# Low parts of four weight blocks: from TensorE products to a GpSimd subtraction and a VectorE addition

## The chip, the cores and the metric

One core of a Trainium2 chip. The metric is the device time of one execution in microseconds (us), the median of several runs. The engines are TensorE (PE in the profile, its weight loads PEld), VectorE (DVE), ScalarE (ACT), GpSimd (POOL) and SyncE (SP), which issues all loads and stores.

## What is computed

Masked attention for 8 batches, 8 heads, 576 tokens, head size 64 (heads 0 to 3 see the last 32 positions, heads 4 to 7 the earlier positions with the same remainder by 32), and then a gated layer on the 512 joined features:

```python
attn = softmax(where(mask, q @ k.T / sqrt(D), -1e9)) @ v
x = attn.transpose(0, 2, 1, 3).reshape(B, S, H * D)
h = np.maximum(x @ w_in, 0.0)                   # 512 -> 1024
conv_out = sum(conv_w[k] * hp[:, k:k + S] for k in range(3))   # along the tokens
gate = 1.0 / (1.0 + np.exp(-conv_out))
return h * gate @ w_out                          # 1024 -> 512
```

The weights `w_in`, `conv_w` and `w_out` come as 64-bit floats.

## The kernel before, in words

**Two-part numbers.** Each operand of the large products is kept as a high part in a short form of fp32 (fp32r) and a low part, the rest. A product is then three TensorE instructions, high times high, low weight times high, high weight times low: `wih`, `wil` (from `w_in`) against `xh`, `xl` (lines 568), and `woh`, `wol` (from `w_out`) against `gh`, `gl` (line 634). Three such instructions of 512 columns are called a triple here.

**Weight blocks.** `convert` (from line 235) brings in the weights in eight blocks, c = 0 to 7: four of `w_in` (c 0 to 3), four of `w_out` (c 4 to 7), each of 1024 words in two halves b = 0, 1. SyncE loads the 64-bit words into a buffer `ws` (two of them, taken in turn). A clamp (line 282, on GpSimd or VectorE), ScalarE's `abs` (283), VectorE's `ts` and `stt` (284, 285) make a fp32 `t` out of the upper words, in place; ScalarE rounds it to the high part `wh` (287); VectorE's `ts` and `stt` (294, 296) make the `tail` out of the lower words in a buffer `wl`. The low part is t - wh + tail, and `SPLIT_W` says for each block how it is formed:

- "a" (lines 307 to 313): op `whole` on TensorE, three products into a PSUM bank (`eye` by t, `negr`, the negative unit matrix, by wh, and `eyer` by the tail), and ScalarE's `evict` to SBUF.
- "q" (lines 315 to 320): op `less` on TensorE, two products (`negr` by wh, `eyer` by the tail), and VectorE's `vadd` (line 319) adds t out of SBUF to the bank and writes the low part.

`SPLIT_W` is "aaqqqaqq": of the last four blocks, 4, 6 and 7 are "q" and 5 is "a".

**Attention.** A unit is one batch and one pair of heads, 32 in all. VectorE and ScalarE do the softmax; VectorE turns its result (line 448, `STREAM_TRANSPOSE`) for the product with v. From unit 4 on, TensorE's scores of unit n (line 370) and values of unit n-1 (line 471) are one op, a `visit`, written here as visit n. ScalarE and VectorE then take `xh` (504) and `xl` (529) out of PSUM.

**The layer.** For each of nine groups g of 512 tokens and each of eight column blocks f, `mm1` makes four triples into a bank, and `conv_gate` follows: ScalarE's `relu` (581), VectorE's scaling or ScalarE's (596, 593), two `conv` (602), ScalarE's `tanh` (605), VectorE's `gate` (606), ScalarE's `gh` (609), and `gl` (611) mostly on GpSimd. Three pairs of buffers, `hs` and `cs`, are taken in turn. `mm2` (634) makes eight triples for each of four output blocks m; output block m needs the low parts of weight block c = 4 + m.

**What sets the order.** All operations are first collected in a list, and `Plan.emit` (line 137) issues them in the order of a list of 2149 numbers written out by hand, `ORDER`. Each engine works in that order. `BANKS` gives the PSUM bank of each use; `FILLS` puts products of zeros ahead of a TensorE operation (line 654, each wide one 512 columns of bf16, each narrow one 256), which have no result. Before, there are 54 wide and 4 narrow ones, of which the last two stand ahead of visit 6.

Of the kernel before, what the change touches and what calls it, by code (L numbers as in the profile page):

```python
# [22 lines left out]
W = 32  # L23
# [4 lines left out]
SPLIT_W = "aaqqqaqq"  # L28
# [11 lines left out]
    "10322312121131300313023013133002101213101003123022131132231032011032302113023132013202133102103230210313023203022230113021332010"  # L40
)
ORDER = [
# [82 lines left out]
]  # L125
FILLS = {
    22: (0, 6, 1), 30: (0, 13, 1), 10: (0, 11, 0), 56: (5, 2, 0), 92: (0, 6, 0), 128: (3, 2, 0), 69: (4, 2, 1), 115: (2, 4, 1), 61: (0, 6, 0),
    317: (5, 2, 0),
}

class Plan:
# [3 lines left out]
    def op(self, engine, kind, fn, reads=(), writes=(), **more):  # L135
        self.ops.append((engine, kind, fn, tuple(reads), tuple(writes), more))
# [10 lines left out]
def tile_banded_attention_gated_mlp(ctx, tc, qkT, vw, w_in, conv, w_out, consts_in, more_in, out):  # L147
# [87 lines left out]
    def convert(src, kind, j):  # L235
# [28 lines left out]
        def block(x, b):  # L264
            return place(x, slice(b, b + 1))

        def four(x):
            return x.rearrange("p (c n) -> p c n", n=C)
# [499 lines left out]
```

## Time and profile before

| | |
|---|---|
| median of 3 runs | 502.88 us (502.09 to 503.33) |
| the profiled execution | 503.48 us |
| its span, first to last instruction | 501.6 us |
| TensorE, VectorE, ScalarE, GpSimd busy | 98%, 73%, 57%, 26% of the span |
| mean granted TensorE clock | 0.996 of full |

A row of a timeline gives the start, the duration, the engine, the line, the operation, the output and inputs by the program's names, the shape, how many instructions are merged in the row, and in brackets how long the engine had been idle and who ended it. TensorE products overlap: a product of 512 columns shows 0.39 us, and the next one starts about 0.23 after it.

### The profile page before, as it was taken

Reading aid. Unit: us, or ns where it says so; the run is one execution under the profiler, and the core shown is the slowest. Engines: PE = TensorE matmul, PEld = TensorE weight load, DVE = VectorE, ACT = ScalarE, POOL = GpSimd, SP = SyncE. Lnnn points to the kernel's source line nnn. Section 1 sums busy time; section 2 is a strip of 40 time slices with the busy share of each in tenths; the row PEclk is TensorE's granted clock in tenths of the full one; section 3 lists DMA queues with packets and bytes.
Section 4 is the critical chain, followed back from the end, with each engine's and each line's share of the span. In section 5 each row is a group of like instructions: output and inputs, shape, how many; then the busy total and the mean of one; then the engine's idle time right before and its main releaser. Section 6 shows DMA issues by size and latency. Waiting matters only on the chain.

```text
span 501.6 us, 15936 instructions
## 1 busy us (share of the span) xinstructions
PE 491.8 (98%) x6935; PEld 396.9 (79%) x6935; DVE 368.5 (73%) x655; ACT 283.4 (57%) x611; POOL 132.8 (26%) x216
## 2 busy tenths in 40 slices
PE   8799999999999999999999999999999999999996
PEld 4467767788888888888888888888888888888896
DVE  2999999877957687599768994888578755743730
ACT  4887687367535753367246653654376527745641
POOL 0200534031311340034303340323114303532430
PEclk9899999999999999999999999999999999999999
DMA  8766435420351314403045125004531120001001
GB/s 315 275 218 195 133 106 208 141 90 37 112 141 54 103 48 169 145 34 116 15 123 182 58 98 172 26 3 162 158 121 50 33 86 1 1 8 70 8 12 74
DMA packets 17350, 51.43 MB, mean 103 GB/s; under 512 B 2048, under 2 KB 2944, under 8 KB 17280
## 3 DMA queue, kind: packets, MB, share of 16 engines
q1 hardware_dynamic: 17280, 50.41, 29.5%
q8 instruction: 54, 0.88, 0.7%
q14 instruction: 16, 0.13, 0.1%
HBM read 40.97 MB, written 9.44 MB: 100 GB/s over the span
## 4 chain that ended last, share of the span: by engine, by line
PE 86%; DVE 7%; ACT 4%; issue 1%; POOL 1%; DVEq 0%; ACTq 0%
PE m L634 38%; PE m L568 36%; PE r L471 5%; PE r L370 4%; DVE misc L602 2%; PE m L654 2%; ACT t L405 1%; ACT t L446 1%; DVE ws L285 1%; ACT wa L283 1%; DVE misc L606 1%; DVE mx L392 1%; DVE wl L296 0%; DVE misc L596 0%; DVE sm L421 0%
## 5 line engine op out<-in xcount | busy, mean ns | idle before, releaser
L602 DVE SCALAR_TENSOR_TENSOR misc<-misc,cw 128x512 f32<-128x512 f32 (+26 forms) x256 | 131.2, 545 | 35.4 <-ACT misc L593 32.5
L634 PE MATMUL m<-gh,woh 128*128 128x512 f32 (+2 forms) x320 | 119.4, 373 | 0.0
L634 PE MATMUL m<-gl,woh 128*128 128x512 f32 (+2 forms) x320 | 117.8, 368 | 0.1
L634 PE MATMUL m<-gh,wol 128*128 128x512 f32 (+2 forms) x320 | 117.8, 368 | 0.0
L611 POOL TENSOR_TENSOR gl<-misc,gh 128x512 fp32r<-128x512 f32 (+1 forms) x70 | 86.1, 1234 | 107.9 <-ACT gh L609 104.1
L568 PE MATMUL m<-xh,wih 128*128 128x512 f32 x288 | 113.9, 395 | 0.0
L568 PE MATMUL m<-xh,wil 128*128 128x512 f32 x288 | 112.3, 390 | 0.0
L568 PE MATMUL m<-xl,wih 128*128 128x512 f32 x288 | 112.3, 390 | 0.0
L634 PEld LDWEIGHTS m<-gl,woh 128*128 128x128 f32 x320 | 60.2, 188 | 11.0 <-POOL gl L611 0.5
L634 PEld LDWEIGHTS m<-gh,woh 128*128 128x128 f32 x320 | 60.1, 188 | 10.3
L634 PEld LDWEIGHTS m<-gh,wol 128*128 128x128 f32 x320 | 60.1, 188 | 9.6
L581 ACT ACTIVATE misc<-m 128x512 f32<-128x512 f32 x72 | 42.5, 596 | 39.2 <-PE m L568 34.5
L593 ACT ACTIVATE misc<-misc,cw 128x383 f32<-128x383 f32 (+15 forms) x122 | 59.7, 523 | 8.2 <-POOL gl L611 4.2
L609 ACT CAST gh<-misc 128x512 fp32r<-128x512 f32 (+1 forms) x72 | 44.2, 618 | 35.1 <-DVE misc L606 34.8
L605 ACT ACTIVATE misc<-misc 128x512 f32<-128x512 f32 (+1 forms) x72 | 44.6, 628 | 33.5 <-DVE misc L602 33.4
L568 PEld LDWEIGHTS m<-xl,wih 128*128 128x128 f32 x288 | 54.1, 188 | 11.9 <-DVE xl L529 0.4
L568 PEld LDWEIGHTS m<-xh,wih 128*128 128x128 f32 x288 | 54.0, 188 | 11.8 <-ACT xh L504 0.2
L568 PEld LDWEIGHTS m<-xh,wil 128*128 128x128 f32 x288 | 54.1, 188 | 10.5
L583 POOL COPY misc<-carry 128x2 f32<-128x2 f32 x64 | 21.7, 347 | 152.2 <-DVE misc L606 91.7
L606 DVE SCALAR_TENSOR_TENSOR misc<-misc 128x512 f32<-128x512 f32 (+1 forms) x72 | 51.9, 725 | 11.7 <-ACT misc L605 11.1
L504 ACT CAST xh<-r 128x576 fp32r<-128x576 f32 (+13 forms) x56 | 23.5, 429 | 37.0 <-PE r L471 31.8
L641 ACT ACTIVATE misc<-m 128x512 f32<-128x512 f32 (+2 forms) x40 | 21.7, 556 | 39.6 <-PE m L634 39.1
(76 smaller groups left out, 494.3 us busy)
## 6 DMA issues: line engine op xcount, KB each, us to landing
qk<-in_dram SPq DMA_DIRECT2D x32, 592.0 KB, 5.0
v<-in_dram SPq DMA_DIRECT2D x32, 384.0 KB, 4.5
ws<-in_dram SPq DMA_DIRECT2D x14, 512.0 KB, 4.8
out_dram<-misc SPq DMA_DIRECT2D x28, 256.0 KB, 2.7
misc<-in_dram SPq DMA_DIRECT2D x2, 512.0 KB, 7.9
out_dram<-misc SPq DMA_DIRECT2D x4, 255.5 KB, 2.1
out_dram<-misc SPq DMA_DIRECT2D x3, 256.5 KB, 2.1
more<-in_dram SPq DMA_DIRECT2D x1, 320.0 KB, 5.2
```

Source lines behind the costliest of these rows:

```text
L471: nc.tensor.matmul(psV[64 * h:64 * h + 64, o:o + n_], v[W * c:W * c + W, h, j], tt[W * c:W * c + W, 64 * NBLK * h + a:64 * NBLK * h + z], ...
L504: op(A, "xh", lambda hi=hi, src=src: nc.scalar.copy(hi, src), ko, [("xh", hp, x) for x in halves], n=z - a)
L568: nc.tensor.matmul(ps, a[:, n, fs], x[:, c, N * x0:N * x0 + N], start=(n == 0 and m == 0), stop=(n == NC - 1 and m == 2))
L581: op(A, "relu", lambda: nc.scalar.activation(out=h[:, 2:N + 2], in_=ps, func=AF.Relu), [kp], [("h", hi)], n=N)
L583: op(G, "gcopy", lambda: nc.gpsimd.tensor_copy(out=h[:, 0:2], in_=carry[:, f, :]), [("carry", f)], [("h0", hi)], lock=True)
L593: op(A, "scale", lambda a=a, z=z: nc.scalar.activation(out=c_[:, a:z], in_=h[:, a + 1:z + 1], func=AF.Copy, scale=w1), kh + ["cw"], (kc if ...
L602: op(V, "conv", lambda k=k, wk=wk, a=a, z=z: nc.vector.scalar_tensor_tensor(out=c_[:, a:z], in0=h[:, a + k:z + k], scalar=wk, in1=c_[:, a: ...
L605: op(A, "tanh", lambda: nc.scalar.activation(out=c_[:, :n], in_=c_[:, :n], func=AF.Tanh, scale=0.5), kc, kc, n=n)
L606: op(V, "gate", lambda: nc.vector.scalar_tensor_tensor(out=c_[:, :n], in0=c_[:, :n], scalar=1.0, in1=h[:, 1:n + 1], op0=ALU.add, op1=ALU.m ...
L609: op(A, "gh", lambda: nc.scalar.copy(row(gh, g, f)[:, :n], c_[:, :n]), kc, [(k, "h") for k in keys], n=n)
L611: op(es, "gl", lambda: se.tensor_tensor(out=row(gl, g, f)[:, :n], in0=c_[:, :n], in1=row(gh, g, f)[:, :n].bitcast(F32), op=ALU.subtract), ...
L634: nc.tensor.matmul(ps, a[:, f, ms], row(y, g, f)[:, tok], start=(f == 0 and n == 0), stop=(f == NF - 1 and n == 2))
```

## The change

`SPLIT_W` becomes "aaqqpppp". For a block with "p", for each half, GpSimd subtracts wh from t into the buffer `wa` (op `wsub`, 512 columns, SBUF to SBUF), and VectorE adds the tail and writes the low part (op `tt`, 512 columns, SBUF to SBUF). No TensorE product, no PSUM bank and no ScalarE eviction is used. Op numbers stay the same, as each half had two operations before and has two now. `ORDER` is another order of the same 2149 numbers, on every engine and for the loads. `BANKS` has 120 entries in place of 128. `FILLS` now gives 91 wide and 5 narrow products of zeros.

```diff
-SPLIT_W = "aaqqqaqq"
+SPLIT_W = "aaqqpppp"
...
-            for b in bs:
+            if SPLIT_W[c] in "pd":
+                for b in bs:
+                    key = (kind, 2 * j + b)
+                    zb, eb = slice(512 * b, 512 * b + 512), [("WA", ia, b)]
+                    de, dn = (nc.gpsimd, G) if SPLIT_W[c] == "p" else (nc.vector, V)
+                    op(dn, "wsub", lambda zb=zb, b=b, de=de: de.tensor_tensor(out=four(af[:, zb]), in0=four(t[:, zb]), in1=block(wh, b).bitcast(F32), op=ALU.subtract),
+                       [("W", i, b), (key, "h")], eb, n=512, lock=True)
+                    op(V, "tt", lambda zb=zb, b=b: nc.vector.tensor_tensor(out=block(wlo, b), in0=four(af[:, zb]), in1=four(tail[:, zb].bitcast(F32)), op=ALU.add),
+                       eb + [("WL", il, b)], [(key, "l")], n=512, lock=True)
+                continue_ = True
+            else:
+                continue_ = False
+            for b in [] if continue_ else bs:
                 key = (kind, 2 * j + b)
                 mi = bank()
                 ps = psM[place_of(mi)]
...
 FILLS = {
-    22: (0, 6, 1), 30: (0, 13, 1), 10: (0, 11, 0), 56: (5, 2, 0), 92: (0, 6, 0), 128: (3, 2, 0), 69: (4, 2, 1), 115: (2, 4, 1), 61: (0, 6, 0),
-    317: (5, 2, 0),
+    22: (0, 12, 1), 30: (0, 17, 1), 10: (0, 11, 0), 56: (0, 10, 0), 69: (2, 1, 0), 82: (0, 15, 0), 370: (1, 1, 0), 331: (4, 4, 0), 195: (1, 1, 0),
+    301: (6, 2, 1), 451: (2, 1, 0), 417: (3, 13, 1), 376: (4, 3, 1),
 }
```

The first number of a `FILLS` entry is the TensorE operation that the zero-products precede: 331 is visit 7, 348 visit 8, 417 and 451 are triples of group 1, 370 and 376 triples of output block 1 of group 0. The parts of the orders that the prediction speaks of, counted from the two lists:

- VectorE, up to the transpose of unit 6 (op 324): the same operations as before and both additions of block 5 (218, 220).
- VectorE, up to the transpose of unit 7 (op 339): these two more; both additions of block 6 (257, 259) and three operations on block 7 (290, 291, 293: `ts`, `stt`, `ts`) now come after it.
- VectorE, from the last addition of block 5 (218) to the transpose of unit 6 (324): a sum, a reciprocal, two scalings, a `ts` of block 6, four `conv`, one `gate`.
- TensorE, up to visit 7: the same operations as before without the splits of blocks 4 and 5. Up to visit 8: also without those of block 6, and six triples of output block 2 (380 to 385) come after it.
- GpSimd: the second `wsub` of block 4 stands behind the clamp of block 5 and a `gl`; both `wsub` of block 5 behind the clamp of block 6, ahead of the `gl` of column block 3; those of blocks 6 and 7 behind all `gl` of group 0.
- SyncE: the loads of units 4 to 13 and of blocks 3, 5 and 7 change places among each other.

## Rows read from the trace of the kernel before

**Rows 1.** The page, busy time, share of the span and instructions of each engine.

```profile
PE 491.8 (98%) x6935; PEld 396.9 (79%) x6935; DVE 368.5 (73%) x655; ACT 283.4 (57%) x611; POOL 132.8 (26%) x216
```

**Rows 2.** By stretch: length, busy us (instructions) of PE, PEld, DVE, ACT, POOL, clock, DMA.

```profile
40.00:65.06 25.06, 24.93 (x370) 19.17 (x357) 24.83 (x42) 17.95 (x43) 7.65 (x9) 1.00 0.51 172
65.06:80.53 15.47, 14.88 (x211) 11.04 (x211) 15.47 (x24) 12.10 (x27) 4.18 (x4) 1.00 0.53 195
80.53:95.51 14.98, 14.87 (x213) 11.83 (x212) 14.88 (x24) 6.77 (x12) 5.19 (x5) 1.00 0.37 109
95.51:497.60 402.09, 402.09 (x5440) 335.19 (x5439) 283.37 (x517) 217.56 (x437) 110.20 (x183) 1.00 0.24 79
```

**Rows 3.** Timeline of TensorE, splits of blocks 4 and 5.

```profile
57.73 0.40 PE L316 MATMUL m<-woh,negr 128*128 128x512 f32 x1
...
58.20 0.40 PE L568 MATMUL m<-xh,wih 128*128 128x512 f32 x1
...
69.34 1.06 PE L309 MATMUL m<-ws,consts 128*128 128x512 f32 x2
...
71.23 0.50 PE L311 MATMUL m<-wl,eyer 128*128 128x512 f32 x1 [0.59 <-DVE wl L296]
...
72.93 0.39 PE L568 MATMUL m<-xh,wih 128*128 128x512 f32 x1
```

**Rows 4.** Timeline of TensorE, zero-products, visits 7 and 8, the last product.

```profile
42.76 0.71 PE L654 MATMUL m<-warm 128*128 128x512 bf16 x3
...
80.53 0.83 PE L370 MATMUL r<-qk 64*32 64x32 f32 x72
81.29 1.12 PE L471 MATMUL r<-tt,v 32*64 32x32 f32 x84
...
95.51 0.34 PE L370 MATMUL r<-qk 64*32 64x64 f32 x16
...
96.49 1.03 PE L471 MATMUL r<-tt,v 32*64 32x2 f32 x80
...
497.54 0.28 PE L634 MATMUL m<-gl,woh 128*128 128x258 f32 x1
```

**Rows 5.** Timeline of VectorE.

```profile
32.64 1.00 DVE L399 TENSOR_SCALAR mx<-mx 128x10 f32<-128x10 f32 x1
...
65.77 2.07 DVE L285 SCALAR_TENSOR_TENSOR ws<-ws,wa 128x1024 int32<-128x1024 int32 x1
...
69.96 1.21 DVE L296 SCALAR_TENSOR_TENSOR wl<-ws,wa 128x1024 fp32r<-128x1024 uint32 x1
...
75.22 0.82 DVE L421 TENSOR_REDUCE sm<-t 128x10 f32<-128x650 f32 x1
...
80.07 0.83 DVE L448 STREAM_TRANSPOSE tt<-t 128x640 f32<-128x640 f32 x1
...
83.44 0.68 DVE L611 TENSOR_TENSOR gl<-misc,gh 128x512 fp32r<-128x512 f32 x1
...
88.37 0.68 DVE L319 TENSOR_TENSOR wol<-ws,m 128x512 fp32r<-128x512 f32 x1
...
92.28 1.22 DVE L285 SCALAR_TENSOR_TENSOR ws<-ws,wa 128x1024 int32<-128x1024 int32 x1
...
93.62 0.68 DVE L294 TENSOR_SCALAR wa<-ws 128x1024 int32<-128x1024 int32 x1
94.22 0.84 DVE L448 STREAM_TRANSPOSE tt<-t 128x640 f32<-128x640 f32 x1
```

**Rows 6.** Groups of instructions of GpSimd, 54 to 86 us (busy, mean ns).

```profile
L611 POOL TENSOR_TENSOR gl<-misc,gh 128x512 fp32r<-128x512 f32 x7 | 9.5, 1365 | 19.7 <-ACT gh L609 19.7
...
L282 POOL TENSOR_SCALAR ws<-ws 128x1024 f32<-128x1024 f32 x2 | 2.8, 1408 | 2.9 <-DMA ws<-in_dram 2.9
```

**Rows 7.** Timeline of GpSimd, the clamp of block 6.

```profile
65.57 1.18 POOL L282 TENSOR_SCALAR ws<-ws 128x1024 f32<-128x1024 f32 x1 [2.94 <-DMA ws<-in_dram]
```

**Rows 8.** The chain that ended last: start, us, what; ten triples.

```profile
116.01 6.80 PE m L568 x30
```

More of the change, by code (lines that the diff above doesn't have):

```diff
@@ L39 @@
 BANKS = (
-    "10322312121131300313023013133002101213101003123022131132231032011032302113023132013202133102103230210313023203022230113021332010"
+    "013200200131032101031322131023112332103211300331300213201023012021300013102331021022310130122132301201121202331232231010"
 )
 ORDER = [
[82 rows of a table removed]
[82 rows of a table added]
 ]
 FILLS = {
-    22: (0, 6, 1), 30: (0, 13, 1), 10: (0, 11, 0), 56: (5, 2, 0), 92: (0, 6, 0), 128: (3, 2, 0), 69: (4, 2, 1), 115: (2, 4, 1), 61: (0, 6, 0),
-    317: (5, 2, 0),
+    22: (0, 12, 1), 30: (0, 17, 1), 10: (0, 11, 0), 56: (0, 10, 0), 69: (2, 1, 0), 82: (0, 15, 0), 370: (1, 1, 0), 331: (4, 4, 0), 195: (1, 1, 0),
+    301: (6, 2, 1), 451: (2, 1, 0), 417: (3, 13, 1), 376: (4, 3, 1),
 }
```

164 rows, old and new, of the table ORDER are left out of this document.

## The prediction

> **What bounds the kernel now.** The page first: TensorE is busy for 98% of the span [rows 1]. That says little about a single stage, so next the busy time by stretch [rows 2]. From 95.51 us on TensorE is never idle (402.09 of 402.09) while VectorE works 283.37 of the same 402.09, some 70%: TensorE alone sets the pace there. From 40 to 95.51 us both are nearly full (24.93 and 24.83 of 25.06; 14.88 and 15.47 of 15.47; 14.87 and 14.88 of 14.98). In that stretch two engines share the bound, and work taken from one of them is a gain only if the other lets it be. All the work that the change touches lies there, apart from its last block.
>
> The TensorE timeline shows what the old way costs: one `less` (two products) starts at 57.73 and the next product at 58.20, 0.47 us; the two `whole` of block 5 last from 69.34 to 72.93, 3.59 us, of which 0.59 is a wait for VectorE's tail [rows 3]. The fences of the argument are the visits: TensorE's visit n does the scores of unit n and the values of unit n-1, and its second half needs the transpose of unit n-1 from VectorE. Visit 7 starts at 80.53 and its values at 81.29, visit 8 at 95.51 and 96.49 [rows 4]; the transposes they need end at 80.07 + 0.83 = 80.90 and 94.22 + 0.84 = 95.06 [rows 5]. So at visit 7 TensorE has 0.39 us in hand, at visit 8 1.43 us.
>
> **The change, part by part.**
>
> *Taken from TensorE.* Six `less` and two `whole`: 6 x 0.47 + 3.59 = 6.4 us. Ahead of visit 7 stand two `less` and both `whole` (4.5 us), between visits 7 and 8 two `less` (0.94), after visit 8 two (0.94).
>
> *Taken from ScalarE.* Two evictions out of PSUM. ScalarE is not full in any stretch [rows 2], so nothing is counted; the cover is VectorE, which is full.
>
> *Given to VectorE.* Eight SBUF additions in place of six additions that read PSUM. The nearest row for the new form, the one subtraction of 512 columns that VectorE does between SBUF tiles, lasts 0.68 us, and the old PSUM addition 0.68 too [rows 5]. Instructions there follow each other 0.08 before the end of the last one (93.62 + 0.68 against 94.22), so an addition occupies 0.60, a `ts` of 1024 words 0.60, an `stt` 1.22 - 0.08 = 1.14. Six swaps cost nothing; the two additions of block 5, which replace ScalarE's evictions, cost 1.20 us of a full engine.
>
> *Given to GpSimd.* Eight subtractions. Seven of the same shape between 54 and 86 us took 1.37 us on average [rows 6], so 11 us in all; GpSimd works 7.65, 4.18 and 5.19 us in the three stretches [rows 2] and has room. In its queue the second subtraction of block 4 stands behind a clamp, and it now frees the buffer into which SyncE loads block 6, where the addition did before; I take that load 1 us later. The two of block 5 stand ahead of the `gl` of column block 3. Both delays end in slack: the clamp that took the load came at 65.57 [rows 7], and VectorE's first instruction on that block stands next to the reduction that starts at 75.22 [rows 5].
>
> *The shared access of VectorE and GpSimd.* At 65.57 GpSimd starts a clamp that lasts 1.18 [rows 7]; VectorE's `stt` that starts at 65.77 lasts 2.07 against 1.22 at 92.28 [rows 5], 0.85 more, so it stood until GpSimd was done. Of the nine long GpSimd instructions in that stretch [rows 6] this is the one large loss. The price of a new subtraction for VectorE lies between 0 (it falls beside VectorE work that reads PSUM) and its whole 1.37; I take 0.85 / 9 = 0.1, the mean over the nine, as they are the nearest rows: the same engine pair in the same stretch. Four subtractions lie ahead of visit 7: 0.4 us.
>
> The Trainium skill (SBUF - State Buffer, "Who interferes with whom") calls the pair of ports that these two engines share an exclusive lock: a VectorE instruction with two SBUF inputs and a GpSimd instruction that reads SBUF exclude each other for the whole instruction, and whichever starts second waits. The row at 65.77 agrees. By it the new additions, which read SBUF twice where the old ones read PSUM, become instructions that can be shut out; it speaks against this change, and what it would make of the time is rival C.
>
> *The new order on VectorE.* Counted from the two orders, the transpose of unit 6 has the same instructions ahead of it plus the two additions of block 5: it ends at 80.90 + 1.20 + 0.4 = 82.50. The transpose of unit 7 has these two more, and five fewer: two additions of block 6 (1.20), two `ts` (1.20) and one `stt` (1.14) are moved behind it: 95.06 + 1.20 - 3.54 + 0.4 = 93.12.
>
> *The new order on TensorE.* Ahead of visit 7 stand exactly the old output and input products, only without the four splits, and with zero-products (L654) put into the space: 4.5 us less work, but the visit cannot run before its transpose. A waiting TensorE product starts 0.06 after VectorE's end (69.96 + 1.21 = 71.17 against 71.23) [rows 3, 5]. So the values of visit 7 start at 82.56, the visit at 82.56 - 0.76 = 81.80, 1.27 us later than now: the removed work is turned into waiting. The same comes out at the low part of block 5: its last addition has 5.45 us of VectorE work between it and that transpose (75.22 to 80.07 and a `ts`), so it ends near 76.3, and the seven triples of 0.68 [rows 8] and four zero-products of 0.23 [rows 4] that follow on TensorE end at 81.8.
>
> From visit 7 to visit 8 TensorE needs 80.53 to 95.51 = 14.98 now; less two `less` (0.94), less six triples that are moved behind visit 8 (6 x 0.68 = 4.08), plus three wide and one narrow zero-product (0.8): 10.76. Visit 8 starts at 81.80 + 10.76 = 92.56; its transpose would allow 93.12 + 0.06 - 0.98 = 92.20. It starts 2.95 us earlier than now, but with 4.08 us of triples put off and 0.94 us still saved.
>
> **The sum.** Now 501.6 - 95.51 = 406.09 us pass from visit 8 to the end (last product at 497.54 [rows 4], then the last store). After the change 406.09 + 4.08 - 0.94 = 409.23, if TensorE stays full, as it does now [rows 2]. The span is 92.56 + 409.23 = 501.8, 0.2 more. The profiled execution took 503.48 for a span of 501.6 and lies 0.6 above the median of 502.88; on the median the forecast is 503.1. The tail, the loads of the first 40 us and the later column groups are the same instructions and are costed at nothing.
>
> **The rivals.** A difference of 0.3%, 1.5 us, is about what a measurement of this kernel tells from no change.
>
> A, the forecast: VectorE's pace up to visit 8 gives the saving back. 503.1, within 501.4 to 504.4. For it: VectorE's 15.47 of 15.47 [rows 2], and that nothing is taken from VectorE.
>
> B: VectorE arrives earlier than its queue shows, because its losses to GpSimd are not in the instructions but in how they meet. The 0.85 at 65.77 and the ten-column instruction at 32.64 that took 1.00 us [rows 5], of which I put 0.8 down to the clamp running then, need not recur in a new order, and the 0.4 counted may not come: 503.1 - 0.85 - 0.8 - 0.4 = 501.0. It decides if visit 7 starts before 80.5.
>
> C: slower, by the shared access. If each of the four subtractions ahead of visit 7 shuts VectorE out for the 0.85 of the worst row, 3.4 in place of 0.4, the time is 503.1 + 3.0 = 506.1; for its whole length, 5.5 in place of 0.4, 508.2. It decides as soon as VectorE loses more than 0.4, since visit 7 waits for it with no slack left. Against it: only one of nine such instructions cost so much.
>
> D: TensorE is the bound from 40 us on after all, and all 6.4 us come off: 496.7. For it, the 0.39 and 1.43 us that TensorE has in hand at the visits now; against it, that 0.39 is used up by 4.5 us removed.
>
> **How the numbers follow.** A 0.42, B 0.26, C 0.28, D 0.04. Faster is B and D, 0.30; same is A, 0.42; slower is C, 0.28. The range reaches from a little below B, 499.8, to between C's two prices, 507.5; D and C's end lie outside, about 2 in 10 with what I have not thought of.
>
> **What would show it.** The L309 to L319 work of the last four blocks gone from TensorE, eight GpSimd subtractions of 1.1 to 1.6 us, VectorE additions near 0.68. Right: VectorE full until about 93, the transpose of unit 6 ending near 82.5 and of unit 7 near 93, visit 7 starting at 81 to 82.5 with zero-products ahead of it, visit 8 near 92.5, and TensorE full after. C would show as VectorE instructions of 1.2 us and more beside the subtractions. Wrong: visit 8 before 91, or TensorE idle after 100 us.

## The result, and the profile after

| | before | after |
|---|---|---|
| median | 502.92 us (4 runs) | 507.44 us (4 runs, 505.17 to 507.88) |
| ratio | | 1.0086, 95% interval 1.0062 to 1.0109 |
| the profiled execution | 503.48 us, span 501.6 | 507.88 us, span 506.1 |

The changed kernel is slower by 0.9%. The time is inside the range given (499.8 to 507.5), but the likeliest case was "no difference", at 503.1. One execution of the third experiment (603.39 us) and one of the last (543.72) had a lower granted clock than the others, 0.75 and 0.85, and the medians of these two leave them out. In the changed kernel's lines everything from L320 on stands 12 lines lower than before: scores L382 and L389, values L483, zero-products L666, transpose L460, triples L580 and L646. The subtraction is L306, the addition L308.

The page of the changed kernel, the busy line and the larger of the two queues that carry instructions:

```profile
PE 495.7 (98%) x6953; PEld 396.4 (78%) x6953; DVE 372.5 (74%) x657; ACT 281.8 (56%) x609; POOL 144.7 (29%) x224
...
q8 instruction: 54, 0.88, 0.7%
```

TensorE has only 18 products more than before [rows 1]: the six `less` and two `whole` are gone, 20 products by their rows, and 38 zero-products came. The second line will matter: 54 packets of kind instruction, 0.88 MB.

By stretch, cut as in [rows 2], and then 70 to 76 us (busy us of PE, PEld, DVE, ACT, POOL, clock, DMA):

```profile
40.00:65.06 25.06, 24.67 (x374) 19.27 (x360) 24.99 (x40) 17.25 (x39) 11.74 (x11) 1.00 0.50 165
65.06:80.53 15.47, 13.75 (x205) 8.71 (x204) 15.36 (x24) 10.16 (x24) 8.81 (x7) 0.89 0.53 189
80.53:95.51 14.98, 14.98 (x273) 11.33 (x272) 13.65 (x22) 7.88 (x15) 7.18 (x7) 1.00 0.13 46
95.51:502.00 406.49, 405.05 (x5412) 336.52 (x5396) 290.47 (x523) 215.96 (x436) 109.77 (x183) 1.00 0.24 80
70.00:72.00 2.00, 2.00 (x15) 1.08 (x16) 1.93 (x3) 1.67 (x4) 0.82 (x1) 0.73 0.38 90
72.00:74.00 2.00, 2.00 (x7) 0.63 (x5) 2.00 (x4) 0.63 (x2) 2.00 (x2) 0.50 0.57 132
74.00:76.00 2.00, 2.00 (x10) 1.11 (x9) 2.00 (x4) 0.98 (x2) 1.94 (x3) 0.92 0.83 291
```

VectorE is full up to visit 7, as before. But in that stretch TensorE is idle for 1.72 us, and its granted clock, which had not left 1.00 there, is 0.89: from 72 to 74 it is 0.50, the lower of the two levels, 1.2 GHz in place of 2.4. The TensorE timeline shows where this begins (the last column is the idle time before, and who ended it):

```profile
66.27 0.34 PE L382 MATMUL r<-qk 64*32 64x64 f32 x16
...
67.25 0.94 PE L483 MATMUL r<-tt,v 32*64 32x2 f32 x71
69.91 0.32 PE L483 MATMUL r<-tt,v 32*64 32x32 f32 x9 [1.72 <-issue]
70.16 0.50 PE L580 MATMUL m<-xh,wih 128*128 128x512 f32 x1
...
70.98 4.75 PE L666 MATMUL m<-warm 128*128 128x512 bf16 x14
75.48 0.49 PE L580 MATMUL m<-xh,wih 128*128 128x512 f32 x1
...
84.56 0.83 PE L382 MATMUL r<-qk 64*32 64x32 f32 x72
85.32 1.11 PE L483 MATMUL r<-tt,v 32*64 32x32 f32 x84
...
94.89 0.34 PE L382 MATMUL r<-qk 64*32 64x64 f32 x16
...
96.34 1.03 PE L483 MATMUL r<-tt,v 32*64 32x2 f32 x80 [0.39 <-DVE tt L460]
```

Visit 6 stops after 71 of its 80 value products. All of these wait for the same transpose, which had let the first 71 through, so the stop is no wait for data; "issue" says that the profile shows nothing that was waited for. Behind it 14 zero-products take 4.5 us (70.98 to 75.48), where at full clock one takes 0.23. The stretches, beside those of the forecast:

| | before | forecast | after |
|---|---|---|---|
| visit 7 starts | 80.53 | 81.80 | 84.56 |
| visit 7 to visit 8 | 14.98 | 10.76 | 10.33 |
| visit 8 to the end | 406.1 | 409.23 | 411.2 |

VectorE in the changed kernel, the rows that answer to [rows 5], and GpSimd's subtractions of blocks 5 and 6, two each:

```profile
57.08 1.53 DVE L614 SCALAR_TENSOR_TENSOR misc<-misc,cw 128x512 f32<-128x512 f32 x1
...
66.21 0.84 DVE L460 STREAM_TRANSPOSE tt<-t 128x640 f32<-128x640 f32 x1
...
70.95 0.68 DVE L308 TENSOR_TENSOR wol<-wa,wl 128x512 fp32r<-128x512 f32 x1
...
72.44 0.89 DVE L618 SCALAR_TENSOR_TENSOR misc<-misc 128x512 f32<-128x512 f32 x1
...
73.79 1.24 DVE L308 TENSOR_TENSOR wol<-wa,wl 128x512 fp32r<-128x512 f32 x1
...
82.84 0.84 DVE L460 STREAM_TRANSPOSE tt<-t 128x640 f32<-128x640 f32 x1
...
93.78 1.63 DVE L453 TENSOR_TENSOR t<-t,sm 128x480 f32<-128x480 f32 x1
95.44 0.84 DVE L460 STREAM_TRANSPOSE tt<-t 128x640 f32<-128x640 f32 x1
```

```profile
71.18 3.31 POOL L306 TENSOR_TENSOR wa<-ws,woh 128x512 f32<-128x512 f32 x2 [3.75 <-DVE wl L296]
...
92.29 2.60 POOL L306 TENSOR_TENSOR wa<-ws,woh 128x512 f32<-128x512 f32 x2 [2.17 <-ACT woh L287]
```

The transpose for visit 7 ends at 83.68, 1.18 later than forecast. But the values of visit 7 start at 85.32, 1.64 after that: VectorE did not hold visit 7 back in this execution, TensorE was late by itself.

### The profile page after: what moved, and what is told of

The parts are those of the page before. It is cut to its first block, busy times and chain, and to the rows that moved or that the text cites. A ratio compares the mean times of both kernels' runs of the same rounds, so it can differ in the third digit from the quotient of the medians.

```text
span 506.1 us, 15965 instructions
## 1 busy us (share of the span) xinstructions
PE 495.7 (98%) x6953; PEld 396.4 (78%) x6953; DVE 372.5 (74%) x657; ACT 281.8 (56%) x609; POOL 144.7 (29%) x224
## 4 chain that ended last, share of the span: by engine, by line
PE 87%; DVE 5%; ACT 4%; DMA 2%; issue 1%; ACTq 0%; DVEq 0%
PE m L646 39%; PE m L580 34%; PE r L483 6%; PE r L382 4%; PE m L666 2%; ACT t L417 1%; DVE misc L614 1%; DMA out_dram<-misc 1%; DMA ws<-in_dram 1%; ACT wa L283 1%; DVE tt L460 0%; ACT t L458 0%; DVE mx L404 0%; ACT misc L653 0%; ACT wih L287 0%
## 5 line engine op out<-in xcount | busy, mean ns | idle before, releaser
L614 DVE SCALAR_TENSOR_TENSOR misc<-misc,cw 128x512 f32<-128x512 f32 (+27 forms) x256 | 131.7, 551 | 37.8 <-ACT misc L605 36.6
L623 POOL TENSOR_TENSOR gl<-misc,gh 128x512 fp32r<-128x512 f32 (+1 forms) x70 | 88.0, 1260 | 117.7 <-ACT gh L621 116.3
L646 PE MATMUL m<-gh,woh 128*128 128x512 f32 (+2 forms) x320 | 119.9, 375 | 0.8 <-ACT misc L593 0.8
L646 PE MATMUL m<-gl,woh 128*128 128x512 f32 (+2 forms) x320 | 117.8, 368 | 0.0
L646 PE MATMUL m<-gh,wol 128*128 128x512 f32 (+2 forms) x320 | 117.7, 368 | 0.0
L580 PE MATMUL m<-xh,wih 128*128 128x512 f32 x288 | 114.7, 398 | 0.2 <-ACT misc L653 0.2
L580 PE MATMUL m<-xl,wih 128*128 128x512 f32 x288 | 112.4, 390 | 0.0
L580 PE MATMUL m<-xh,wil 128*128 128x512 f32 x288 | 112.3, 390 | 0.0
L646 PEld LDWEIGHTS m<-gh,woh 128*128 128x128 f32 x320 | 60.1, 188 | 11.7 <-ACT misc L593 1.5
L646 PEld LDWEIGHTS m<-gl,woh 128*128 128x128 f32 x320 | 60.1, 188 | 10.2
L646 PEld LDWEIGHTS m<-gh,wol 128*128 128x128 f32 x320 | 60.1, 188 | 9.7
L605 ACT ACTIVATE misc<-misc,cw 128x193 f32<-128x193 f32 (+15 forms) x122 | 59.4, 523 | 13.3 <-DMA out_dram<-misc 6.9
L580 PEld LDWEIGHTS m<-xh,wih 128*128 128x128 f32 x288 | 54.1, 188 | 12.0 <-ACT misc L653 0.7
L580 PEld LDWEIGHTS m<-xl,wih 128*128 128x128 f32 x288 | 54.0, 188 | 11.8 <-DVE xl L541 0.2
L580 PEld LDWEIGHTS m<-xh,wil 128*128 128x128 f32 x288 | 54.1, 188 | 10.6
L618 DVE SCALAR_TENSOR_TENSOR misc<-misc 128x512 f32<-128x512 f32 (+1 forms) x72 | 53.0, 742 | 10.6 <-ACT misc L617 9.8
L621 ACT CAST gh<-misc 128x512 fp32r<-128x512 f32 (+1 forms) x72 | 44.2, 618 | 16.4 <-DVE misc L618 15.6
L595 POOL COPY misc<-carry 128x2 f32<-128x2 f32 x64 | 18.6, 300 | 113.2 <-DVE misc L618 54.0
```

What stands on the lines that cost most here:

```text
L580: nc.tensor.matmul(ps, a[:, n, fs], x[:, c, N * x0:N * x0 + N], start=(n == 0 and m == 0), stop=(n == NC - 1 and m == 2))
L605: op(A, "scale", lambda a=a, z=z: nc.scalar.activation(out=c_[:, a:z], in_=h[:, a + 1:z + 1], func=AF.Copy, scale=w1), kh + ["cw"], (kc if ...
L614: op(V, "conv", lambda k=k, wk=wk, a=a, z=z: nc.vector.scalar_tensor_tensor(out=c_[:, a:z], in0=h[:, a + k:z + k], scalar=wk, in1=c_[:, a: ...
L618: op(V, "gate", lambda: nc.vector.scalar_tensor_tensor(out=c_[:, :n], in0=c_[:, :n], scalar=1.0, in1=h[:, 1:n + 1], op0=ALU.add, op1=ALU.m ...
L621: op(A, "gh", lambda: nc.scalar.copy(row(gh, g, f)[:, :n], c_[:, :n]), kc, [(k, "h") for k in keys], n=n)
L623: op(es, "gl", lambda: se.tensor_tensor(out=row(gl, g, f)[:, :n], in0=c_[:, :n], in1=row(gh, g, f)[:, :n].bitcast(F32), op=ALU.subtract), ...
```

## The experiments

Two theories to begin with. One: the stop in visit 6 and the clock behind it are the loss, and the stop is TensorE waiting for its own instructions. The packets of queue 8 are of 16384 bytes each, and there are 54 of them for 13906 TensorE instructions (weight loads and products counted together), one per some 257; one left at 67.43 and took 1.14 us. The Trainium skill (Runtime: NRT & Kernel Launch, "Instruction fetch mechanics") says that an engine's instructions are fetched in blocks of 16 KiB, 256 instructions, while it works on those before, and that this is mostly hidden. The packets here agree with the size; by this theory the stop is a place where it is not hidden. The other theory: the new way of forming, or the new order, costs the time by the sharing between GpSimd and VectorE.

**14 zero-products fewer, early.** All later TensorE instructions move forward by 28.

```diff
-    82: (0, 15, 0),
+    82: (0, 1, 0),
```

> The changed kernel with 14 fewer zero-products, all ahead of one TensorE operation of the first 40 us (1 in place of 15), so that every later TensorE instruction has a number lower by 28. In the changed kernel TensorE stops at 67.97 us, in the middle of the values of visit 6, for 1.94 us, named issue, with nothing waited for; a packet of 16384 bytes in the queue of kind instruction is on its way just then, and the granted clock is 0.50 to 0.73 in the 4 us after. Theory (instruction stop): TensorE had run out of instructions, because that visit of 305 short instructions begins 146 instructions behind a multiple of 256. With visit 6 at 118, where the visits of the old kernel lay without a stop, the stop is gone, the clock is 1.00 from 66 to 76 us, and the time is 505 to 506.5 us, 1 to 2.5 less than the changed kernel's 507.4. Rival (sharing between GpSimd and VectorE, or the new order itself): the 14 products lie in waiting time, so nothing changes: 507.4 within 0.5, even if the stop goes.

508.77 us, ratio 1.0126 (1.0112 to 1.0139): slower, not faster. The timeline of TensorE and the clock from 95 to 100 say why:

```profile
82.96 0.83 PE L382 MATMUL r<-qk 64*32 64x32 f32 x72
...
94.29 0.84 PE L483 MATMUL r<-tt,v 32*64 32x2 f32 x58
96.93 0.48 PE L483 MATMUL r<-tt,v 32*64 32x48 f32 x22 [1.80 <-issue]
```

```profile
95.00:100.00 5.00, 3.20 (x39) 2.50 (x29) 3.41 (x6) 1.74 (x3) 0.00 (x0) 0.72 0.41 152
```

Visit 6 ran through, the clock was 1.00 from 66 to 76, and visit 7 came at 82.96, 1.6 earlier. But the shift had carried the stop into visit 8, where it cost as much, with a lower clock behind it. The expectation had placed visit 6 alone.

**The old kernel with 26 instructions more.**

```diff
-    22: (0, 6, 1), 30: (0, 13, 1),
+    22: (0, 6, 1), 30: (0, 0, 27),
```

> The old kernel with the 13 wide and 1 narrow zero-products ahead of one early TensorE operation replaced by 27 narrow ones: about the same TensorE time, but 13 products, so 26 TensorE instructions, more. Visit 6 then begins 139 instructions behind a multiple of 256 in place of 113. Theory (instruction stop): the old kernel gets the stop that only the changed one had, of 1.5 to 2 us in the middle of the values of visit 6, named issue, with a 16384 byte instruction packet under way, and a lower granted clock behind it; time 504 to 506.5 us, 1 to 3.5 more than 502.9. Rival (the stop belongs to the new order or to the new GpSimd work): no stop, 502.9 within 0.5.

506.72 us, 1.0084 (1.0071 to 1.0098). The old kernel, with none of the change in it, becomes as slow as the changed one, and its visit 6 shows the stop:

```profile
66.36 0.97 PE L471 MATMUL r<-tt,v 32*64 32x2 f32 x74
69.28 0.31 PE L471 MATMUL r<-tt,v 32*64 32x32 f32 x6 [1.95 <-issue]
```

A second stop, 1.47 from start to start, lay at 111.06. The clock stayed at 1.00 here. So the stop needs neither GpSimd's new work nor the new order, only a certain number of instructions ahead.

Counted over the traces, the stops named issue inside a visit lie, within three instructions, at number 189 + 255 k: k = 5 and 9 in this run, 9 in the changed kernel, 12 and 44 in the run before, 9 in the third, 5, 12, 22, 30 and 44 in the fourth; those of the later runs (2, 9, 12, 22 and 44) fit too. In the unedited old kernel instruction 2484 (k = 9) lies 334 behind the start of visit 6, which has 320. In the stops of over 1.4 us that were followed up (the changed kernel's, the first experiment's in visit 8, this run's in visit 6, the fourth's at 368.93) TensorE went on 2.4 to 2.5 us after the packet had left (67.43 and 69.91 in the changed kernel), and within a visit 255 instructions last only some 1.4 us (320 in 1.80). When the packet leaves is not fixed: in other visits TensorE passed such a number without a stop or with one of 0.5. What sets that is open.

**The subtractions on VectorE.**

```diff
-SPLIT_W = "aaqqpppp"
+SPLIT_W = "aaqqdddd"
```

> The changed kernel with the eight subtractions on VectorE in place of GpSimd; order, banks, zero-products and all TensorE instructions are the same. VectorE gets 4 more instructions of about 0.65 us ahead of visit 7 and loses what GpSimd's subtractions cost it (0.56 at 73.79, 0.15 at 72.44, about 1 at 93.78). Theory (sharing costs little, VectorE's own work sets the pace, and the stop of TensorE in visit 6 stays): 2.6 minus 0.7 later at visit 7 and 1.3 more at visit 8: 508.5 to 511 us. Rival (a GpSimd subtraction shuts VectorE out for its whole length, 1.3 to 1.7 us each): VectorE gains more than it gets, 504 to 506.5 us.

507.50 us, 1.0096 (1.0081 to 1.0110): neither range holds. The stop shrank to 0.35 us, since the values of visit 6 had first waited 0.98 for VectorE, while the packet was under way, and the clock stayed up. VectorE's longer work and the smaller stop nearly cancel: visit 6 to visit 7 takes 17.95 us in place of 18.29. The comparison was repeated below without the stop.

**The new way of forming in the old order.** `ORDER`, `BANKS` (less eight uses) and `FILLS` of the kernel before, and

```diff
-    30: (0, 13, 1),
+    30: (0, 5, 17),
```

> The changed way of forming the low parts of the last four blocks, but in the old order, with the old banks (less the eight uses that no longer exist) and the old zero-products, of which one early group has 5 wide and 17 narrow in place of 13 wide and 1 narrow, which keeps every visit away from the place at which the changed kernel stops. Theory (VectorE sets the pace to visit 8; the way of forming gains nothing, and the loss of the changed kernel is the stop and what the new order does): two additions ahead of visit 7 and four ahead of visit 8, 2.4 us, plus some tenths of sharing, against 6.4 us less on TensorE that end in waiting: visit 8 at 96.5 to 98, and 502.5 to 504.5 us. Rival 1 (the way of forming itself is what costs, by sharing): 506 us or more. Rival 2 (TensorE's work is what counts in the old order): 497 to 500 us.

515.54 us, 1.0264 (1.0251 to 1.0277): far over the forecast range, in Rival 1's. TensorE's waits from 40 to 110 us (us in total, times, longest):

```profile
PE r L382 <- DVE xl L541: 5.6, 1, 5.6
PE r L483 <- DVE tt L460: 2.4, 1, 2.4
PE m L646 <- DVE wol L308: 2.1, 2, 1.9
```

In the old order the subtractions stand where the splits stood for TensorE, and VectorE, whose queue is full, waits 2.2 us for GpSimd's two of block 4; what stands behind those additions is late, `xl` first, for which the scores of visit 6 wait 5.6. During that wait the granted clock falls, to 0.50 from 65.25 to 75.50. There are stops named issue in later visits too, the longest of 2.30 at 368.93. So the new order belongs to the new way of forming. The opposite pair, the old way in the new order, was not tried.

**The stop taken away.** Both places where zero-products stand are changed, so that visit 6 has its numbers from the first experiment and visits 7 and later those of the changed kernel. The number of instructions is that of the changed kernel.

```diff
-    82: (0, 15, 0),
+    82: (0, 1, 0),
-    417: (3, 13, 1),
+    417: (3, 0, 28),
```

> The changed kernel with its zero-products placed so that no visit is at a place where TensorE runs out of instructions: 14 wide ones fewer ahead of one operation of the first 40 us, and 13 wide and 1 narrow ones behind visit 6 replaced by 28 narrow ones of the same total time. The number of TensorE instructions is the same as in the changed kernel; only those between the two places have other numbers. The stops named issue seen so far lie at numbers 189 + 255 k (after 9 and 12 times 255 in the changed kernel and in the first of these runs, 5 and 9 in the old kernel with 26 instructions more), when TensorE gets there within 270 to 310 instructions of the start of a visit. Here visit 6 has none there, as in the first run, and visits 7 and 8 stand as in the changed kernel. Theory (the stop and the low clock behind it are the loss; for the rest the saving is given back to VectorE as forecast): no stop, visit 7 at 82.5 to 83.2, visit 8 at 93 to 93.6, 503 to 504.7 us. Rival 1 (it costs something else too): 505.5 to 507.5. Rival 2 (the saving shows once the stop is gone): under 502.

505.16 us, 1.0057 (1.0035 to 1.0080): between the theory's 503 to 504.7 and Rival 1's 505.5 to 507.5. No visit has a stop; it falls among the zero-products, 0.69 us. Visit 6 to visit 7 takes 16.58 us (67.50 to 84.08) in place of 18.29 (66.27 to 84.56), 1.71 less, and visit 7 to 8 10.40:

```profile
67.50 0.34 PE L382 MATMUL r<-qk 64*32 64x64 f32 x16
...
71.34 3.01 PE L666 MATMUL m<-warm 128*128 128x256 bf16 x26 [0.69 <-issue]
...
84.08 0.83 PE L382 MATMUL r<-qk 64*32 64x32 f32 x72
...
94.48 0.34 PE L382 MATMUL r<-qk 64*32 64x64 f32 x16
```

But visit 6 came at 67.50, and the first 40 us show another loss:

```profile
16.09 0.39 PE L666 MATMUL m<-warm 128*128 128x512 bf16 x1
17.47 1.17 PE L321 MATMUL m<-misc,consts 128*128 128x512 f32 x2 [0.99 <-DVE misc L285]
18.16 0.72 PE L322 MATMUL m<-wih,negr 128*128 128x512 f32 x1
20.37 0.79 PE L323 MATMUL m<-wl,eyer 128*128 128x512 f32 x1 [1.49 <-DVE wl L296]
```

```profile
20.00:25.00 5.00, 4.63 (x85) 2.85 (x86) 4.51 (x10) 4.62 (x16) 2.61 (x3) 0.50 0.52 183
```

Where the 14 zero-products were taken out, TensorE waits, and the clock is 0.50 just behind; in the changed kernel it is 1.00 from 20 to 25. The first experiment, with the same early edit, has the same two waits (1.10 and 1.50), but there the clock stayed at 1.00 and visit 6 came at 66.38. So the edit brings the waits, but not in every execution the lower clock and the late visit 6. In the next run and in the one with the scalings on ScalarE, which have the same edit, the clock is 0.66 from 20 to 25, and visit 6 starts at 65.91 and 65.38.

**The same without the stop, subtractions on VectorE.** `SPLIT_W` as above.

> The run before, without the stop, with the eight subtractions on VectorE in place of GpSimd. Theory (VectorE's own work sets the pace up to visit 8, and sharing costs it less than the work): 4 subtractions of 0.65 ahead of visit 7, 2.6, less some 0.9 that GpSimd's four cost VectorE there; 1 to 2.2 us more than the run before, 504.2 to 506.5. Rival (GpSimd's subtractions shut VectorE out for more than VectorE would need itself): the same as the run before or less, 502 to 503.7.

507.10 us, 1.0105 (1.0081 to 1.0129), 1.9 us over the run before, above the 504.2 to 506.5 expected but by the difference that the theory gave, 1 to 2.2. What GpSimd's subtractions cost VectorE by sharing is less than what VectorE pays for doing them.

**The old order, subtractions on VectorE.**

> The run with the old order and the new way of forming took 515.5 us; its VectorE waited 2.2 us for GpSimd's two subtractions of block 4, which stood in the old order behind the copies and the low parts of the gated values in GpSimd's queue. Here the eight subtractions are on VectorE, in the old order; the instructions of TensorE are the same as in that run, and so are the places where it may run out of them. Theory (in the old order the subtraction comes late, and VectorE, which then waits, is the bound): no wait for GpSimd, 4 times 0.65 more work ahead of visit 7, 2 to 5 us less than 515.5: 510.5 to 513.5. Rival (the new way of forming is what the old order cannot bear, wherever the subtraction is done): 515 or more.

513.84 us, 1.0229 (1.0206 to 1.0252): 1.7 less than with GpSimd, just short of the range; the two ran on different chips, and their intervals just touch. GpSimd's lateness is a small part of what the old order loses; the rest was not taken apart. Stops named issue in later visits, up to 1.72 from start to start, and a granted clock of 0.66 from 66 to 76 belong to it.

**Scalings from VectorE to ScalarE,** in the run without the stop.

```diff
-SCALE = "vaavvvvv"
+SCALE = "vaaaaaaa"
```

> The run without the stop, with the scaling of the last five column blocks of group 0 on ScalarE in place of VectorE: 0.48 less VectorE work at each of five places, three of them ahead of visit 7 and all ahead of visit 8, and 0.6 more on ScalarE, which is idle for some 4 of the 10 us ahead of 76. Theory (VectorE's queue is what visits 7 and 8 wait for): visit 7 1 to 1.5 earlier, visit 8 1.5 to 2.2 earlier, 501.3 to 503 us. Rival 1 (TensorE or the chain through ScalarE takes over): as without this edit, 503 to 504.7. Rival 2 (ScalarE becomes late): 505 or more.

506.58 us, 1.0084 (1.0060 to 1.0109). This is in Rival 2's range, but so was the run without this edit (505.16), and the two intervals overlap: that the edit costs time is not shown. The trace shows the lateness that Rival 2 names. Visit 6 to visit 7 takes 16.4 us (65.4 to 81.8) in place of 16.6, but then VectorE waits for ScalarE, here from 76 to 96 us:

```profile
DVE misc L614 <- ACT misc L605: 2.3, 1, 2.3
DVE sm L433 <- ACT t L428: 1.1, 1, 1.1
```

The last scaling stood behind ten instructions of ScalarE, the transpose for visit 7 was late, the values started 1.86 us after the last score (from start to start), and the clock was 0.66 from 85 to 90.

**The pair once more, on one chip.** The changed kernel unedited, and the run without the stop.

> The changed kernel once more, unedited, on the same chip and beside the same runs as the next one, so that the two differ in nothing but the places of the zero-products. Theory (the stop in visit 6 and what follows it): the stop is there again, at the same instruction, number 2484; 1.5 to 3 us more than the next run. Rival (the stop is an accident of one profiled execution, and the difference to the run without it was one of chips): within 0.7 us of the next run.

> The run without the stop once more, for the pair with the run before: theory 504 to 505.5 us and no stop in a visit; rival within 0.7 us of the run before.

506.86 us, 1.0081 (1.0068 to 1.0094), against 504.36 us, 1.0035 (1.0019 to 1.0050): 2.5 us apart, and the intervals do not touch. The changed kernel's stop was at the same instruction:

```profile
66.83 0.34 PE L382 MATMUL r<-qk 64*32 64x64 f32 x16
...
67.81 0.94 PE L483 MATMUL r<-tt,v 32*64 32x2 f32 x71
69.95 0.32 PE L483 MATMUL r<-tt,v 32*64 32x32 f32 x9 [1.20 <-issue]
...
84.59 0.83 PE L382 MATMUL r<-qk 64*32 64x32 f32 x72
```

The run without it spreads from 502.95 to 507.15. Its profiled execution is the longest of its twelve, 507.15, and has the early loss again: clock 0.57 from 20 to 25, visit 6 at 68.94.

```profile
68.94 0.34 PE L382 MATMUL r<-qk 64*32 64x64 f32 x16
...
85.50 0.83 PE L382 MATMUL r<-qk 64*32 64x32 f32 x72
```

From there to the end of its span it needs 505.4 - 68.94 = 436.5 us, as much as the old kernel (501.6 - 65.06 = 436.5); the first run without the stop needed 505.0 - 67.50 = 437.5. The changed kernel needed 506.1 - 66.27 = 439.8 in its first profile, but only 504.2 - 66.83 = 437.3 in this one, the fastest of its five. From visit 6 to visit 7 this pair takes 17.76 us with the stop (66.83 to 84.59) and 16.56 without (68.94 to 85.50), 1.20 apart; where the rest of the 2.5 us between the medians arises, the traces do not show.

**Four scalings on ScalarE.**

```diff
-SCALE = "vaavvvvv"
+SCALE = "vaaaaaav"
```

> The run without the stop, with the scaling of four column blocks of group 0 on ScalarE in place of VectorE (not of the fifth, whose scaling came 2.3 us late when it stood behind ten instructions of ScalarE and made the transpose of visit 7 late). Theory (VectorE's queue is what visits 7 and 8 wait for): 1.8 us less of it ahead of visit 7, of which up to 1.1 may come back as a wait for ScalarE's exponential; visit 7 at 81.5 to 82.3, 0.7 to 1.5 us less than the run without the stop, 503.5 to 504.5. Rival (ScalarE's lateness eats it): no difference of more than 0.5.

504.57 us, 1.0036 (1.0019 to 1.0054): no difference to the run without the stop, as the rival had it. From visit 6 to 7 it takes 16.43 us in place of 16.58 and 16.56, so less VectorE work is worth some 0.1 there. TensorE's idle times that remain in that stretch are 0.31 for ScalarE, 0.37 for VectorE's addition and 0.36 named issue, none for the transpose. Between the two visits stand 28 narrow and 6 wide zero-products; whether the run would gain with fewer of them was not tried.

**One part of the change alone,** blocks 6 and 7 in the old order.

```diff
-SPLIT_W = "aaqqqaqq"
+SPLIT_W = "aaqqqapp"
-    30: (0, 13, 1),
+    30: (0, 7, 13),
```

> One part of the change alone: in the old kernel, in its old order, only the last two weight blocks get GpSimd's subtraction and VectorE's addition; the first two of the four are formed as before. The number of VectorE instructions is unchanged, TensorE loses four splits of 0.47, 1.9 us; six products more ahead of an early operation and eight fewer later keep the visits away from the places of the stop. Theory (in the old order TensorE and VectorE both have under 1.5 us in hand at visits 7 and 8, and GpSimd's subtraction of 1.3 comes later than a split of 0.47): 0 to 1 us gained on TensorE, as much lost by VectorE's waits, 501.5 to 504 us. Rival 1 (TensorE's saving counts when VectorE gets no more work): 500 to 501.5. Rival 2 (the late subtractions stop the queues as in the run with all four blocks in the old order): 506 or more.

506.07 us, 1.0053 (1.0036 to 1.0069): slower, where 501.5 to 504 was expected, and at Rival 2's bound of 506. No usable trace stands behind this number, so whether the late subtractions or another stop costs it is open.

No kernel that ran beats the kernel before.

## Why the prediction was right or wrong

The range held; the case did not. A difference of 0.3% or less had 0.42, and what came is a loss of 0.9% by a mechanism that none of the four cases names. Rival C has nearly this time, 506.1 to 508.2, but for another reason. That the range held is luck: it was drawn so far up for Rival C's sake, and the time lies 0.06 us below its end.

**The step that failed** is the one that lets TensorE run at its pace wherever its data are there: "Ahead of visit 7 stand exactly the old output and input products, only without the four splits, and with zero-products (L654) put into the space". The zero-products were counted by their time alone. They and the splits that went also move the number of each later instruction, and so the place where TensorE has to wait for instructions, into visit 6. That is shown by moving it: out of visit 6 and into visit 8, into the old kernel's visit 6, and out of all visits. That TensorE waits for instructions there is inferred from the numbers and the packets; the profile names no cause. From visit 6 to visit 7 the stop and the clock behind it cost 1.71 us in the first pair of traces and 1.20 in the second. On one chip the medians with and without the stop lie 2.5 us apart.

**Taken from TensorE, and turned into waiting**: right. Without the stop visit 6 to 7 takes 16.6 us, where 65.06 to 81.80 was forecast, 16.7; visit 7 to 8 10.4 against 10.76; visit 8 to the end 410.5 and 409.5 in the two executions (505.0 - 94.48; 505.4 - 95.88) against 409.23. That the saving comes back as waiting is shown so far as the old kernel and the changed one without the stop take nearly the same time from visit 6 on, 436.5 us against 436.5 and 437.5. In the first experiment, where visit 6 has no stop, the transpose ends at 82.88 + 0.83 = 83.71 and the values of visit 7 start at 83.77: VectorE does hold the visit back, by the 0.06 that was forecast.

**Given to VectorE**: right. The addition lasts 0.68, as forecast from the nearest rows [rows 5].

**The shared access**: right in kind, its size open. The term was 0.4 us ahead of visit 7, and the 0.85 of the old order's worst row stood in the forecast already. In the changed kernel that row does not recur, but at 57.08 a `conv` lasts 1.53 in place of 0.74 beside a clamp, at 73.79 an addition 1.24 in place of 0.68 and at 72.44 a `gate` 0.89 in place of 0.68 beside subtractions. The transpose for visit 7 ends at 83.68 and not at 82.50, which would give some 1.6 for the whole term (0.4 + 1.18). But the transpose for visit 6, ahead of block 5's subtractions, already ends at 66.21 + 0.84 = 67.05, and in the old kernel at 65.84:

```profile
65.00 0.84 DVE L448 STREAM_TRANSPOSE tt<-t 128x640 f32<-128x640 f32 x1
```

So 1.21 us, as much as the whole lateness, was there before, and 1.6 is no measured size of the term.

The addition at 73.79 falls under the second subtraction, which ends at 71.18 + 3.31 = 74.49, and lasts 0.54 beyond that: it stood until GpSimd was done, as the Trainium skill's lock says (SBUF - State Buffer, "Who interferes with whom"). The addition at 70.95 had begun before the first subtraction, and lasts 0.68. Block 6's subtractions, which the forecast counts at nothing ahead of visit 8, cost more: the scaling of the softmax ahead of that transpose (L453, at 93.78) lasts 1.63, until 0.52 after the end of the second, and TensorE then waits 0.39 for the transpose. The changed kernel's second trace has this too (1.62). In the first experiment and in both runs without the stop, VectorE and GpSimd meet differently there, and the same scaling lasts 0.78. So a subtraction costs what VectorE happens to have beside it, far from Rival C's whole length each: doing them on VectorE cost 1.9 us more.

**Rival B** fell: in all edits of the changed kernel whose visit 6 has no stop, visit 7 starts at 81.78 or later, not before 80.5. **Rival D** fell: no run comes near 496.7.

**TensorE stays full after visit 8**: nearly. It is idle for 1.44 of 406.49 us, 0.39 of it the wait at visit 8 and 0.80 one wait for ScalarE behind 331.83, where the old kernel has none [rows 2]. From start to start this place took 1.19; in three other runs with the new order it took 1.16, 0.66 and 0.55, and in the others it did not show.

**Visit 6** was taken to stay at 65.06. It starts at 66.27; the new order puts two triples more and two splits fewer ahead of it, 1.36 - 0.94 = 0.4, and the rest is lateness that I did not foresee. The 14 more zero-products ahead of it are not the reason, since the first experiment takes as many out and has visit 6 at 66.38. What the change costs once the stop is gone, 1.5 to 2.6 us by the medians of the two runs, contains this and the early loss that some executions with the edit have; the two were not separated.

## What to carry to other kernels

Where TensorE runs hundreds of very short products in a row, its instructions must arrive too: a stop named issue in the middle of a row of products that all have their data is the sign, and adding or removing instructions well ahead of it, here 26 or 28, moves it. So an edit that changes the number of instructions is measured at two or three such offsets before its own worth is judged. Work that leaves one of two full engines is worth only what the other lets through, and the order written for one division of work does not fit another.

## What the runs showed of the hardware

- TensorE stops, as far as numbers and packets tell, for its own instructions: the long stops are 1.20 to 2.08 us of idle time in the middle of a visit, at instruction numbers a multiple of 255 apart, with 54 packets of 16384 bytes for 13906 instructions, and 2.2 to 2.5 us pass from the packet's start to the next product.
- A stop of that kind was followed by a granted clock of 0.50 to 0.73 for some 4 us in the changed kernel, and of 0.72 in the 5 us around it in the first experiment; behind the 1.95 us in the old kernel it stayed at 1.00. What makes the difference is open.
- 26 instructions more, for the same columns of zero-products, made the old kernel 0.84% slower.
- A VectorE instruction that began under a GpSimd subtraction lasted until 0.52 to 0.54 us after it: an addition 1.24 us in place of 0.68, the softmax's scaling 1.63 in place of 0.78.
